# Two units' loads issued later, around the copies of odd values 20, in a fused attention and MLP kernel

## The chip, the cores and the metric

The kernel runs on one core of a Trainium2 chip. The metric is the device time of one execution in microseconds, as the median of several runs. One execution was also recorded by the profiler; its instructions, waits and transfers are what the profile and the trace show.

## The reference

The program computes sliding-window attention and then a two-layer perceptron over its output:

```python
scores = scale * np.matmul(q, k.transpose(0, 1, 3, 2))     # B, H, S, D = 8, 8, 576, 64
mask = np.abs(pos[:, None] - pos[None, :]) <= 32
scores = np.where(mask, scores, -1000000000.0)
attn = softmax(scores)
x = np.matmul(attn, v)            # -> (B * S, H * D) = (4608, 512)
h = x @ w_in                      # (512, 2048)
g = h * (1.0 / (1.0 + np.exp(-1.702 * h)))
out = g @ w_out                   # (2048, 512), float32
```

## The kernel before

**Units and tiles.** The 4608 rows are cut into 36 units of 128 rows (shifted by 32 for the queries) and 9 tiles of 512 rows, four units each. A unit goes through attention: its queries and keys are transposed, the scores are formed on TensorE (PE), exponentiated on ScalarE (ACT), masked on VectorE (DVE, `band`), multiplied with the values on PE (`values`), and divided by the row sums on DVE (`norm`), which gives x. A tile of four units then goes through both layers. Both layers use seven products in place of eight for a 2 by 2 split of the matrices (a Strassen scheme), so DVE forms sums of blocks: `x_sums` (xs) from the transposed x before layer 1, `g_sums` (gs) before layer 2.

**Where the data come from.** `fetch(u)` issues on POOL's queue (GpSimd) the loads of unit u's queries, unit u+1's keys and unit u+1's values, converting float32 to bfloat16 on the way; a load that crosses the end of a batch entry is two transfers. `turn(u)` issues on SP's queue the transposes by DMA of unit u's queries and unit u+1's keys. `odd_v(u)` copies on POOL the values into a second buffer, shifted by 64 rows: one copy reads unit u's values, the other unit u+1's. `x_T(u)` issues on SP the transpose of unit u's x. Finished rows of the output are stored from SP. Each queue works in the order in which its instructions are issued; an instruction whose data or buffer isn't ready holds back all behind it.

There are 5 buffers for staged queries, 5 for staged keys, 9 for values (`ve`), 5 for shifted values (`vo`) and 7 each for transposed queries and keys (`qT`, `kT`).

**The order.** The order on every engine is written out by hand. After an opening that treats the first tiles, the kernel alternates `front(t)` and `back(t)`. `front(t)` begins with the scores of units 4t+4 and 4t+5, goes on with layer 2 of an earlier tile, forms xs for tile t and ends with the scores of the two other units. `back(t)` has four groups n = 0 to 3, each of which calls `turn`, `fetch`, in groups 1 and 3 `values`, `norm` and `x_T` of two units, then `odd_v`, and then a group of layer 1 (`l1_group`, products 1, 7, 6, 2, 5, 4, 3) with layer-2 matmuls between its products. With u = 4t + 4, group n of `back(t)` turns unit u+n+4, fetches unit u+n+5 and copies the odd values of unit u+n+4. So in `back(2)` and `back(3)` (third and fourth tile, t = 2 and 3):

| group | before: turn | before: fetch | before: odd_v |
|---|---|---|---|
| (2, 2) | 18 | 19 | 18 |
| (2, 3) | 19 | 20 | 19 |
| (3, 0) | 20 | 21 | 20 |
| (3, 1) | 21 | 22 | 21 |

The first product that needs xs is product 7 of the tile's first group. The transposed x of units 14 and 15 belongs to the fourth tile, that of 18 and 19 to the fifth.

Of the kernel before, what the change touches and what calls it, by code (L numbers as in the profile page):

```python
# [26 lines left out]
class _Kernel:  # L27
# [706 lines left out]
    @staticmethod  # L734
    def do(fs, n=99):
        for _ in range(min(n, len(fs))):
            fs.pop(0)()
# [29 lines left out]
    def back(self, t):  # L767

        more = t + 1 < self.NT
        do, l2 = self.do, self.l2  # L770
        u = 4 * t + 4
        bands = [lambda i=i: self.band(u + i) for i in range(4)] if more else []
        dv = bands[0:2]
        for n in range(4):
            self.turn(u + n + 4)
            self.fetch(u + n + 5)
            if t == 2 and n in (1, 3):
                self.values(u + n - 1, "t")
                self.norm(u + n - 1)
                self.x_T(u + n - 1)  # L780
            elif more and n in (1, 3):
                do(l2, self.AHEAD[n][0])
                self.values(u + n - 1, "AC")
                self.norm(u + n - 1)
                if u + n < self.NU - 1:
                    self.x_T(u + n - 1)
                self.values(u + n, "t")
                self.norm(u + n)
                self.x_T(u + n)
                do(l2, self.AHEAD[n][1])  # L790
            if u + n + 4 < self.NU:
                self.odd_v(u + n + 4, self.nc.gpsimd)

            key = ("first", n) if t == 2 else ("last", n) if not more else n
            share = dict(zip((1, 7, 2, 4), self.SHARES.get(key, (3, 3, 5, 5))))

            def fill(i):
                do(l2, share[i])
                self.l2eng = self.nc.scalar
                if t == 2 and n in (1, 3) and i == 7:  # L800
                    self.values(u + n, "t")
                    if n == 3:
                        self.norm(u + n)
                        self.x_T(u + n)
                if i == 4:
                    do(dv, 2 if (t, n) == (2, 2) else 99)

            def side(i):
                if (t, n, i) == (2, 1, 0):
                    self.norm(u + n)  # L810
                    self.x_T(u + n)
                else:
                    do(dv, 1)

            self.l1_group(t, n, fill, side)
            dv += bands[2:4] if n == int(t == 2) else []
            dv += self.g_sums(t, 2 * n, 2)
        return dv
# [132 lines left out]
```

## Time and profile before

| | |
|---|---|
| median of 3 runs | 284.54 us (283.01 to 285.44) |
| profiled execution, its own time | 286.76 us |
| its span, first to last instruction | 285.0 us |
| granted clock of TensorE | 0.997 |
| busy: PE, DVE, ACT, POOL | 94%, 74%, 69%, 47% |
| read from HBM, written | 36.83 MB, 9.44 MB |

PE is TensorE's matmuls, PEld its weight loads, which overlap them. A row of a timeline gives the start, the duration, the engine, the line of the code, what is written and read, and in brackets how long the engine sat idle before and what it waited for. SPq and POOLq are the issues of transfers; a transfer lands some microseconds after its issue. A row of a window gives for each engine the busy time and, in brackets, the number of instructions, then the granted clock, the share of the DMA engines and the rate in GB/s.

### The profile page before, as it was taken

What the parts mean: (1) busy time and instruction counts of PE and PEld (TensorE: products, weight loads), DVE (VectorE), ACT (ScalarE), POOL (GpSimd) and SP (SyncE); (2) the same over time, 40 slices, a digit from 0 to 9 for tenths busy, and PEclk for the clock granted to TensorE, in tenths of its full rate; (3) what the DMA queues carried; (4) which work ended last, traced back from release to release, by engine and by line L of the source; (5) the groups of instructions that cost most, each with busy time, mean ns of one, the idle gap of its engine ahead of it and who ended that gap; (6) DMA issues with size and microseconds to landing.
All of it is one profiled execution on the core that took longest, in us unless ns stands there. A gap on an engine that the chain in (4) does not pass through costs nothing.

```text
span 285.0 us, 8889 instructions
## 1 busy us (share of the span) xinstructions
PE 269.0 (94%) x3648; PEld 221.8 (78%) x3648; DVE 212.3 (74%) x492; ACT 195.7 (69%) x343; POOL 133.4 (47%) x199
## 2 busy tenths in 40 slices
PE   1979999999999977999899999999999999999995
PEld 1568657776888865888788888888888888888883
DVE  3465697996987876797779787978788878945731
ACT  2586994899886594667866796689658865568411
POOL 8894785999696770738073908470310000000000
PEclk9999999999999999999999999999999999999998
DMA  8999999999999999999999999999923040201033
GB/s 89 168 205 198 178 207 159 187 121 156 170 133 138 211 124 179 117 163 145 174 112 199 153 177 65 183 158 198 147 58 74 24 113 20 74 2 74 2 110 114
DMA packets 150265, 37.61 MB, mean 132 GB/s; under 512 B 138064, under 2 KB 145872, under 8 KB 150224
## 3 DMA queue, kind: packets, MB, share of 16 engines
q0 software_dynamic: 106656, 18.42, 96.4%
q1 hardware_dynamic: 43120, 18.10, 36.8%
q8 instruction: 28, 0.46, 0.7%
q10 hardware_dynamic: 448, 0.52, 0.6%
q14 instruction: 13, 0.11, 0.2%
HBM read 36.83 MB, written 9.44 MB: 162 GB/s over the span
## 4 chain that ended last, share of the span: by engine, by line
PE 85%; DMA 6%; DVE 4%; ACT 2%; issue 1%; POOL 1%; ACTq 0%; DVEq 0%; POOLq 0%
PE h L70 37%; PE o L70 36%; DMA xT<-x 6%; PE pv L70 4%; PE sc L70 4%; DVE x L328 1%; PE tp L177 1%; DVE xs L388 1%; PE tp L244 1%; ACT kq L67 1%; POOL kq L152 1%; PE tp L344 0%; PE tp L356 0%; ACT L680 0%; PE tp L201 0%
## 5 line engine op out<-in xcount | busy, mean ns | idle before, releaser
L459 ACT ACTIVATE g<-h 128x512 f16<-128x512 f32 x128 | 72.2, 598 | 35.8 <-PE h L70 35.5
L222 POOL COPY vo<-ve 64x264 int32<-64x264 int32 x71 | 33.2, 468 | 65.1 <-PE pv L70 53.0
L70 PEld LDWEIGHTS <-g 128*128 128x128 f16 x576 | 54.5, 98 | 10.1
L70 PE MATMUL h<-xs,a 128*128 128x256 f16 x384 | 57.6, 272 | 2.6 <-DVE xs L388 1.8
L70 PEld LDWEIGHTS <-a 128*128 128x128 f16 x512 | 49.3, 98 | 12.8 <-DVE xs L388 3.7
L70 PE MATMUL o<-w,g 128*128 128x256 f16 (+1 forms) x320 | 55.0, 294 | 0.0
L70 PE MATMUL h<-xT,w 128*128 128x256 f16 (+1 forms) x368 | 53.6, 277 | 0.0
L70 PEld LDWEIGHTS <-w 128*128 128x128 f16 x496 | 47.7, 98 | 7.4
L70 PEld LDWEIGHTS <-gs 128*128 128x128 f16 x384 | 36.7, 98 | 4.8 <-issue 0.2
L290 ACT ACTIVATE p<-sc 128x512 bf16<-128x512 f32 x72 | 37.1, 616 | 3.5 <-PE sc L70 3.3
L70 PE MATMUL o<-b,g 128*128 128x256 f16 x256 | 38.3, 273 | 0.0
L70 PE MATMUL o<-b,gs 128*128 128x256 f16 x256 | 37.7, 273 | 0.0
L211 POOL DMA_DIRECT2D ve<-in_v_dram x40 | 34.3, 868 | 7.1 <-DMA w<-in_moe_w_out_dram 3.1
L472 DVE TENSOR_TENSOR h<-h,s 128x512 f32<-128x512 f32 x32 | 22.4, 699 | 19.5 <-PE h L70 19.3
L67 ACT COPY h<-h 128x512 f32<-128x512 f32 x32 | 18.7, 586 | 17.6 <-PE h L70 17.3
L328 DVE TENSOR_TENSOR x<-pv,rec 128x256 f16<-128x256 f32 (+1 forms) x52 | 27.4, 527 | 1.8
L141 POOL DMA_DIRECT2D qst<-in_q_dram x35 | 28.0, 803 | 1.3 <-issue 0.9
L478 DVE TENSOR_TENSOR h<-h,s 128x512 f32<-128x512 f32 x32 | 22.4, 699 | 6.2 <-PE h L70 5.9
L141 POOL DMA_DIRECT2D kst<-in_k_dram x31 | 26.5, 858 | 0.8 <-DMA w<-in_moe_w_out_dram 0.8
L298 DVE TENSOR_TENSOR p<-p,mask 128x1024 bf16<-128x1024 bf16 x32 | 22.8, 714 | 0.3 <-ACT p L290 0.3
L67 ACT COPY s<-h 128x512 f32<-128x512 f32 x32 | 19.0, 594 | 4.0 <-PE h L70 2.9
L70 PE MATMUL h<-xs,w 128*128 128x256 f16 x128 | 19.2, 273 | 0.0
(87 smaller groups left out, 339.7 us busy)
## 6 DMA issues: line engine op xcount, KB each, us to landing
out_dram<-o_sb SPq DMA_DIRECT2D x33, 256.0 KB, 4.6
ve<-in_v_dram POOLq DMA_DIRECT2D x32, 128.0 KB, 6.9
kst<-in_k_dram POOLq DMA_DIRECT2D x25, 128.0 KB, 6.8
qst<-in_q_dram POOLq DMA_DIRECT2D x21, 128.0 KB, 5.8
w<-in_moe_w_out_dram POOLq DMA_DIRECT2D x4, 512.0 KB, 11.2
w<-in_moe_w_in_dram POOLq DMA_DIRECT2D x3, 512.0 KB, 9.1
qst<-in_q_dram POOLq DMA_DIRECT2D x7, 96.0 KB, 6.3
kq<-in_q_dram POOLq DMA_DIRECT2D x2, 256.0 KB, 5.9
```

Of the source, the lines that this page charges most:

```text
L67: (eng.copy if eng is self.nc.scalar else eng.tensor_copy)(out, in_)
L70: self.nc.tensor.matmul(out, lhsT, rhs, start=start, stop=stop, skip_group_check=True)
L141: self.nc.gpsimd.dma_start(t[off:off + n], src[b, :, s:s + n, :].rearrange("h s d -> s h d"))
L152: self.nc.gpsimd.dma_start(self.stage["first"][0:n // j, :, at:at + j], src[0, :, lo:lo + n, :].rearrange("h (p j) d -> p h j d", j=j))
L211: self.nc.gpsimd.dma_start(t[off:off + n, :, :self.D], self.v[b, :, s:s + n, :].rearrange("h s d -> s h d"))
L222: eng.tensor_copy(*((words(vo[64:128]), words(self.ve[u % 9][64:128])), (words(vo[0:64]), words(nxt)))[i])
L290: self.nc.scalar.activation(p[:, eo].rearrange("k h s -> k (h s)"), sc[eo], AF.Exp, scale=self.scale)
L298: (eng or self.nc.vector).tensor_mul(pv, pv, msk.to_broadcast([128, 8, 2, SQ]))
L328: dve.tensor_mul(x[:, 4 * at:4 * (at + n), :].rearrange("p (b h) d -> p b h d", b=n), acc[:, :, :, :D], r.to_broadcast([128, n, 4, D]))
L459: act.activation(g[:, f, 256 * half:256 * half + 256], bank.rearrange("p (i n) -> p i n", i=2), AF.Gelu_apprx_sigmoid)
L472: dve.tensor_add(e, b, s7)
L478: dve.tensor_add(c, b, s7)
```

## The change

The loads of `fetch(20)`, issued in the last group of `back(2)`, are issued in the first group of `back(3)`, right ahead of the copies of `odd_v(20)`. Those of `fetch(21)` stay in that group, but go from ahead of these copies to behind them. `turn(20)` is written in the second group of `back(3)` in place of the first.

```diff
         for n in range(4):
-            self.turn(u + n + 4)
-            self.fetch(u + n + 5)
+            if (t, n) == (3, 1):
+                self.turn(20)
+            if (t, n) != (3, 0):
+                self.turn(u + n + 4)
+            if (t, n) not in ((2, 3), (3, 0)):
+                self.fetch(u + n + 5)
...
+            if (t, n) == (3, 0):
+                self.fetch(20)
             if u + n + 4 < self.NU:
                 self.odd_v(u + n + 4, self.nc.gpsimd)
+            if (t, n) == (3, 0):
+                self.fetch(21)
```

The order on POOL before and after (each fetch being three to five transfers, each odd_v two copies):

```
before: odd_v(18) fetch(20) odd_v(19) fetch(21) odd_v(20) fetch(22) odd_v(21)
after:  odd_v(18) odd_v(19) fetch(20) odd_v(20) fetch(21) fetch(22) odd_v(21)
```

The order of the instructions on PE, DVE, ACT and SP is the same before and after.

## The prediction

> **What bounds the kernel now.** I read the page first (engines, the slices of the clock and of the DMA engines, the queues), then the chain that ended last, then the timelines of PE, POOL and SP around the fourth tile, and last the times to landing of single transfers.
>
> ```profile
> span 285.0 us, 8889 instructions
> PE 269.0 (94%) x3648; PEld 221.8 (78%) x3648; DVE 212.3 (74%) x492; ACT 195.7 (69%) x343; POOL 133.4 (47%) x199
> PEclk9999999999999999999999999999999999999998
> DMA  8999999999999999999999999999923040201033
> q0 software_dynamic: 106656, 18.42, 96.4%
> q1 hardware_dynamic: 43120, 18.10, 36.8%
> ```
>
> TensorE is busy for 94% of the span at the full granted clock, so time can be won only where it waits. The DMA engines are taken almost without a break until three quarters of the span. The loads that POOL issues (queue 0) and the transposes and stores that SP issues (queue 1) share them.
>
> The kernel goes through its tiles at a nearly fixed pace, so I compare the same stretch in four tiles: from the first score matmuls of front(t) to the first matmul of product 7, which needs the sums xs of the tile's transposed x. The rows below are the fourth to the seventh tile (t = 3 to 6).
>
> ```profile
> 100.47:109.93 9.46, 6.12 (x137) 4.97 (x137) 4.99 (x13) 6.58 (x11) 4.77 (x7) 1.00 2.07 148
> 132.10:138.66 6.56, 5.91 (x137) 4.87 (x137) 4.39 (x12) 6.50 (x12) 2.85 (x4) 1.00 2.53 131
> 160.82:166.56 5.74, 5.74 (x137) 4.96 (x137) 4.90 (x14) 5.71 (x11) 2.81 (x5) 1.00 2.57 164
> 188.48:194.30 5.82, 5.82 (x138) 5.05 (x138) 5.02 (x14) 5.79 (x11) 2.57 (x3) 1.00 2.31 134
> ```
>
> The same 137 matmuls take 5.74 us where nothing is late. In the fourth tile they take 3.72 us more (9.46 - 5.74), in the fifth 0.82 us more. That is all that this change could remove: 4.5 us. What is late is seen in the timelines of PE and DVE, in the chain, and in the landing of the transpose whose issue lies in 100.5 to 101 us:
>
> ```profile
> 105.42 0.44 PE L70 MATMUL sc<-qT,kT 64*64 64x64 bf16 x22 [1.56 <-DMA kT<-kst]
> 109.93 0.61 PE L70 MATMUL h<-xs,a 128*128 128x256 f16 x4 [1.78 <-DVE xs L388]
> 109.45 0.43 DVE L388 TENSOR_TENSOR xs<-xT 128x512 f16<-128x512 f16 x1 [4.23 <-DMA xT<-x]
> ...
> 100.33 9.03 DMA xT<-x
> 129.87 8.21 DMA xT<-x
> ...
> xT<-x SPq DMA_TRANSPOSE x1, 9.0
> ```
>
> First a score waits 1.56 us for the transposed keys of unit 20, then product 7 waits 1.78 us for xs, whose input xT(15) was issued at 100.33 and landed 9.03 us later, at 109.36. The fifth tile has the same wait, smaller: xT(19), issued at 129.87, lands at 138.08.
>
> **The change.** No operation is added or removed; on PE, DVE, ACT and SP the order stays the same (turn(20) and turn(21) were neighbours on SP already). Only POOL's order changes: fetch(20), three issues, goes behind the two copies of odd_v(19), and fetch(21), five issues, behind the two copies of odd_v(20). POOL and SP before:
>
> ```profile
> 92.47 0.88 POOL L141 DMA_DIRECT2D qst<-in_q_dram  x1
> 94.21 0.89 POOL L211 DMA_DIRECT2D ve<-in_v_dram  x1
> 95.14 0.41 POOL L222 COPY vo<-ve 64x264 int32<-64x264 int32 x1
> 96.82 0.40 POOL L222 COPY vo<-ve 64x264 int32<-64x264 int32 x1 [1.28 <-DMA ve<-in_v_dram]
> 97.34 0.88 POOL L141 DMA_DIRECT2D qst<-in_q_dram  x1
> 98.20 1.39 POOL L141 DMA_DIRECT2D kst<-in_k_dram  x2
> 99.55 1.40 POOL L211 DMA_DIRECT2D ve<-in_v_dram  x2
> 101.00 1.23 POOL L222 COPY vo<-ve 64x264 int32<-64x264 int32 x2
> 102.21 1.36 POOL L141 DMA_DIRECT2D qst<-in_q_dram  x2
> 105.74 0.88 POOL L211 DMA_DIRECT2D ve<-in_v_dram  x1 [1.28 <-DMA qst<-in_q_dram]
> 115.26 0.86 POOL L222 COPY vo<-ve 64x264 int32<-64x264 int32 x2 [8.64 <-PE pv L70]
> ...
> 104.54 1.48 SPq L235 DMA_TRANSPOSE qT<-qst  x1
> 109.42 3.00 SPq L235 DMA_TRANSPOSE kT<-kst  x1
> 116.27 2.56 SPq L340 DMA_TRANSPOSE xT<-x  x2
> 119.69 2.16 SPq L493 DMA_DIRECT2D out_dram<-o_sb  x2
> 121.95 1.59 SPq L235 DMA_TRANSPOSE qT<-qst  x1
> 128.56 2.56 SPq L340 DMA_TRANSPOSE xT<-x  x2
> ```
>
> The issues at 92.47 to 95.1 are fetch(20), those from 97.34 fetch(21), those from 102.21 to 106.6 fetch(22). The copies at 95.14 and 96.82 are odd_v(19), the pair at 101.00 odd_v(20), the pair at 115.26 odd_v(21).
>
> **POOL, step by step.** The second copy of odd_v(19) still waits for v(20), loaded by fetch(19), until 96.82. So fetch(20) takes the place that fetch(21) had: q at about 97.3, k at 98.2, v at 99.1, done at 100.0. The first copy of odd_v(20) follows at once, but the second needs v(21), issued only 0.9 us before. Now POOL waits for a load that used to have a head start. Before, v(21) was issued at 94.21 and the pair at 101.00 took 1.23 us in place of 0.86, so it landed near 101.8, 7.6 us after its issue. Its time after the change is bounded by the quickest and the slowest v load near by (windows 146.5 to 147.4 and 100.5 to 101 us):
>
> ```profile
> ve<-in_v_dram POOLq DMA_DIRECT2D x1, 128.0 KB, 5.5
> ve<-in_v_dram POOLq DMA_DIRECT2D x1, 64.0 KB, 9.4
> ```
>
> I take 6.5 us, nearer the quick end since one unit's loads are under way in place of three: v(21) lands at 105.6, the copy ends at 106.0, fetch(21) runs from 106.0 to 109.7 (0.88 + 1.39 + 1.40) and fetch(22) to about 112.8. odd_v(21) was held until 115.26 by the value matmuls of unit 16 (8.64 us of idle). That idle time is the cover: POOL is back in step with 2.4 us to spare, or with none if TensorE comes as much earlier. By the bounds, fetch(21) starts between 105.0 and 108.9.
>
> **What the fourth tile wins.** While xT(14) and xT(15) are under way, queue 0 holds the 3 transfers of fetch(20) in place of up to 12 (3, 5 and 4 of fetch 20, 21 and 22, less those already landed). The time of xT(15) is bounded by 9.0 us (no relief) and by the transposes at 203 to 206 us, where no loads run:
>
> ```profile
> xT<-x SPq DMA_TRANSPOSE x1, 3.5
> xT<-x SPq DMA_TRANSPOSE x1, 7.0
> ```
>
> The second row is xT(23), issued within the window 158.2 to 159 us with one unit's loads around it and transposes of turns ahead of it, the state that the change makes. I take 7.0: landing at 107.3 in place of 109.36, so 2.1 us. The score's wait for kT(20) goes with the same relief. TensorE would then arrive 1.56 + 1.78 = 3.3 us earlier and wait for the last 1.3. Won up to here: 2.1 us, between 0 and 3.7.
>
> By the Trainium skill, page "DMA: Bandwidth & Descriptors", section "Queues, rings and completion order", each DMA engine goes round-robin between the queues it has work for. Taken alone this says that a shorter queue 0 does not help a transpose, only an empty one does, and by it the sum would be near 1 us; this would speak against most of the gain and stands as a rival below. The rows above (7.0 beside one fetch, 9.0 beside three) do not decide it, as the stores and turns around them differ too.
>
> **What the fifth tile gives back.** q(21) now lands near 113 and k(22), whose second half is issued at about 107.6, later than that. SP is in order: turn(21) waits for them, and behind it stand xT(16), xT(17), two stores, turn(22), turn(23), and then xT(18) and xT(19), which the fifth tile waits for. SP had 3.85 us of idle here (109.42 + 3.00 to 116.27), which hides the first part. The bounds for k (windows 88.5 to 91 and 98 to 99 us), and a row between (117.8 to 118.5 us, where fetch(23) and transposes run):
>
> ```profile
> kst<-in_k_dram POOLq DMA_DIRECT2D x1, 128.0 KB, 5.2
> kst<-in_k_dram POOLq DMA_DIRECT2D x2, 64.0 KB, 9.3
> kst<-in_k_dram POOLq DMA_DIRECT2D x1, 128.0 KB, 7.1
> ```
>
> With 7.1, k(22) lands at 114.7. From there SP needs 1.4 for kT(22), 2.7 for the xT pair, 1.1 for the stores (half the 2.16, an issue under load), and 6.6 for two turns (121.95 to 128.56): xT(18) goes out at about 126.5, 11.8 us after k(22), in place of 128.56. That is 2.1 us earlier, the same as TensorE has won, so the fifth tile's own 0.8 us stays and nothing is lost. The point at which it decides: k(22) landing at 116.8 gives all of it back. Later tiles ran without a wait (5.74, 5.82) and keep what is handed on.
>
> **Sum.** 2.1 us at the fourth tile, about 0.1 of the fifth tile's wait: 2.2 us. The profiled execution took 286.76 us with a span of 285.0, 2.2 above the median of 284.54 of the runs shown. 286.76 - 2.2 = 284.5 of its own time; against the median, 284.54 - 2.2 = 282.3 us.
>
> **Rivals.** (A) The relief is larger. Transposes fall to 5 or 6 us, both waits of the fourth tile and that of the fifth vanish: 3.72 + 0.82 = 4.5, 280.0 us. For it: with no loads they land in 3.5. Against it: the rows with loads beside the transpose are 7.0 and 9.0.
>
> (B) The change moves the loads but not the transposes. xT(14) and xT(15) still run beside fetch(20), which sits just where fetch(21) sat, and queue 0 is empty only from about 96.8 to 97.3 and for as short a time near 106. At twice the pace there (3.5 us alone, 7.0 beside loads), xT(15) comes at most 1 us earlier: 283.6 us. By the round-robin rule cited above this is the likely course. For it: the exchange is one fetch for another at the very time when the transposes go out.
>
> (C) Slower: the wait moves to SP. Place: turn(21), behind the late fetch(21), with xT(18) and xT(19) queued after it. With the slow bounds, v(21) in 9.4 us and k(22) in 9.3, k(22) lands at 119.8, xT(18) goes out at 131.6, 3.0 us later than now, and the fifth tile's wait grows by it whatever the fourth has won: 287.5 us. It decides from 116.8 on. For it: four fetches then follow each other from 106 to 121 us, and fetch(22)'s v row already shows POOL held 1.28 us by an earlier load. Against it: the slow times belong to a queue with three fetches in it, and at 99 to 107 there is one.
>
> **How the numbers follow.** Forecast 0.52, A 0.16, B 0.12, C 0.20. The forecast's own range is 1.0 to 3.4 us won, 281.1 to 283.5, as xT(15) takes 8.0 to 5.6 us. A change of 1%, 2.85 us, is about what a measurement of this kernel can tell from none. Not quite half of the forecast lies beyond it, since its two largest terms (7.0 and 7.1 us) each carry over a microsecond: 0.24 faster, 0.28 within. A is faster, B within, C slower but for 0.04. Faster 0.40, within 0.44, slower 0.16. The range of 280.2 to 286.2 leaves out the far end of A and of C.
>
> **What would show it.** In the changed profile: q(20) issued on POOL at about 97.3, a copy of L222 ended by a DMA of ve at about 105.6, fetch(21) behind it, fetch(22) done before 114. xT(15) landing at 107.3, the two PE waits of 1.56 and 1.78 us gone or under 1.3 together; the fourth tile's stretch near 7.4 us in place of 9.46. On SP kT(22) near 114.7, xT(18) near 126.5, and the fifth tile's stretch still near 6.5. Wrong if xT(15) still takes 9 us (B), or if the fifth tile's stretch grows beyond 8 us because SP stood at turn(21) (C).

## The result, and the profile after

| | before | after |
|---|---|---|
| median of 18 runs each | 284.58 us | 283.32 us |
| ratio, 95% interval | | 0.9959 [0.9941, 0.9977] |
| profiled execution, its own time | 286.76 us | 283.51 us |
| its span | 285.0 us | 281.7 us |

The changed kernel is faster by 0.41% in the ratio, 1.3 us between the medians; the forecast was 2.2 us (282.3). The two profiled executions differ by 3.3 us. Why these are not the same number is half of what the experiments had to find.

The page after, and the same stretch as before, from the first scores of front(t) to product 7, for the fourth to the seventh tile. The columns of the second view are the stretch, its length, then the busy time of PE, PEld, DVE, ACT and POOL, the clock, the DMA share and GB/s:

```profile
span 281.7 us, 8889 instructions
PE 268.9 (95%) x3648; PEld 222.5 (79%) x3648; DVE 212.4 (75%) x492; ACT 195.6 (69%) x343; POOL 132.0 (47%) x199
```

```profile
100.54:106.29 5.75, 5.75 (x138) 4.97 (x138) 5.43 (x14) 5.61 (x10) 1.40 (x3) 1.00 1.32 172
128.19:135.45 7.26, 6.11 (x137) 5.02 (x137) 4.32 (x12) 6.58 (x12) 3.52 (x5) 1.00 2.09 146
157.61:163.35 5.74, 5.74 (x137) 4.98 (x137) 4.90 (x14) 5.71 (x11) 2.81 (x5) 1.00 2.39 146
185.25:191.00 5.75, 5.75 (x138) 4.98 (x138) 4.91 (x14) 5.72 (x11) 2.44 (x3) 1.00 2.66 134
```

In this execution the fourth tile's wait is gone altogether: 9.46 us became 5.75. The fifth tile's wait has grown: 6.56 became 7.26. PE's busy time is the same (269.0 and 268.9), so the whole difference is waiting. In the chain that ended last only one transfer is left of the two shown before:

```profile
125.78 9.09 DMA xT<-x
```

It is the transpose of unit 19's x, and it is now slower than before the change (8.21).

POOL and SP after the change:

```profile
95.72 0.40 POOL L222 COPY vo<-ve 64x264 int32<-64x264 int32 x1 [0.20 <-DMA ve<-in_v_dram]
96.23 0.88 POOL L141 DMA_DIRECT2D qst<-in_q_dram  x1
...
104.88 0.50 POOL L222 COPY vo<-ve 64x264 int32<-64x264 int32 x1 [5.57 <-DMA ve<-in_v_dram]
105.39 0.88 POOL L141 DMA_DIRECT2D qst<-in_q_dram  x1
...
112.16 0.86 POOL L222 COPY vo<-ve 64x264 int32<-64x264 int32 x2
```

```profile
97.01 3.34 SPq L340 DMA_TRANSPOSE xT<-x  x2
...
111.55 1.19 SPq L235 DMA_TRANSPOSE kT<-kst  x1
112.84 2.62 SPq L340 DMA_TRANSPOSE xT<-x  x2
...
124.47 2.68 SPq L340 DMA_TRANSPOSE xT<-x  x2
```

fetch(20) starts at 96.23, behind the copy that waits for v(20). The second copy of odd_v(20) then waits 5.57 us for v(21), and fetch(21) follows at 105.39 in place of 97.34. POOL is back in step at 112.16, without idle time.

The travel (issue to landing) of kT(20), which SP issues just ahead of xT(14), before and after:

```profile
kT<-kst SPq DMA_TRANSPOSE x1, 8.0
kT<-kst SPq DMA_TRANSPOSE x1, 4.7
```

It landed at 105.38 before and at 100.40 after, 5.0 us earlier; xT(15) landed at 109.36 and 104.93, 4.4 us earlier. So most of what xT(15) wins has been won by the transposes ahead of it on SP's queue, those of turn(18) and turn(19) from 92 to 98 us, beside which the loads of fetch(20) ran before the change.

### The profile page after: what moved, and what is told of

The parts are those of the page before. It is cut to its first block, busy times and chain, and to the rows that moved or that the text cites. A ratio compares the mean times of both kernels' runs of the same rounds, so it can differ in the third digit from the quotient of the medians.

```text
span 281.7 us, 8889 instructions
## 1 busy us (share of the span) xinstructions
PE 268.9 (95%) x3648; PEld 222.5 (79%) x3648; DVE 212.4 (75%) x492; ACT 195.6 (69%) x343; POOL 132.0 (47%) x199
## 4 chain that ended last, share of the span: by engine, by line
PE 89%; DVE 3%; DMA 3%; ACT 2%; issue 1%; POOL 1%; POOLq 0%; DVEq 0%
PE o L70 38%; PE h L70 38%; PE sc L70 5%; PE pv L70 4%; DMA xT<-x 3%; DVE x L328 1%; PE tp L177 1%; PE tp L244 1%; ACT kq L67 1%; POOL kq L152 1%; ACT p L290 1%; PE tp L356 0%; ACT L680 0%; PE tp L344 0%; DVE xs L388 0%
## 5 line engine op out<-in xcount | busy, mean ns | idle before, releaser
L222 POOL COPY vo<-ve 64x264 int32<-64x264 int32 x71 | 31.8, 448 | 65.0 <-PE pv L70 45.4
```

Source lines behind the costliest of these rows:

```text
L222: eng.tensor_copy(*((words(vo[64:128]), words(self.ve[u % 9][64:128])), (words(vo[0:64]), words(nxt)))[i])
```

## The experiments

Two questions: where did the profile's 3.3 us go in the median, and by what mechanism does the place of a load move a transpose on another queue? The table collects all profiles. "Travel" is the time from issue to landing; the last two columns are the time from the first scores of one front(t) to those of the next, for the fourth and the fifth tile (27.65 us where nothing waits).

| kernel | fetch(20) from | behind v(20)'s landing | fetch(21) from | xT(15) travel | xT(19) travel | 4th tile | 5th tile | ratio |
|---|---|---|---|---|---|---|---|---|
| before | 92.47 | no | 97.34 | 9.0 | 8.2 | 31.63 | 28.72 | |
| b_again | 94.38 | no | 99.14 | 9.1 | 6.8 | 31.27 | 27.64 | |
| after | 96.23 | yes | 105.39 | 6.6 | 9.1 | 27.65 | 29.42 | 0.9959 |
| a_again | 98.96 | yes | 106.68 | 6.0 | 8.3 | 27.64 | 29.63 | |
| e1_only20 | 98.35 | yes | 100.95 | 6.6 | 7.7 | 27.70 | 27.64 | 0.9915 |
| e2_only21 | 93.87 | no | 106.51 | 8.1 | 8.6 | 29.16 | 29.74 | 0.9996 |
| e5_between | 96.37 | no | 101.70 | 8.7 | 6.5 | 30.82 | 27.64 | 0.9991 |
| e7_behind_v20 | 99.54 | yes | 102.55 | 5.8 | 8.3 | 27.72 | 28.49 | 0.9944 |
| e3_swap45 | 98.11 | yes | 107.57 | 7.3 | 5.0 | 29.57 | 27.64 | 0.9925 |
| e8_after_24 | 97.48 | yes | 106.47 | 6.7 | 5.9 | 28.02 | 27.63 | 0.9896 |
| e4_only20_24 | 99.87 | yes | 102.46 | 6.1 | 7.5 | 27.64 | 27.64 | 0.9908 |
| e6_only20to32 | 98.05 | yes | 100.64 | 5.9 | 7.0 | 27.65 | 27.64 | 0.9909 |

**Both kernels profiled once more (b_again, a_again).** No edit.

> The kernel before, unchanged, profiled once more. Theory 1 (the first profile of before caught an execution with a longer wait than usual in the fourth tile): its stretch from the first scores of front(3) to product 7 is well under the 9.46 us of the first profile, about 7.0 to 7.5, its own time near 284.6. Theory 2 (the first profile was typical, and the change gives its gain back later in most executions): the stretch is again 9.0 to 9.7, with xT(15) 9 us on its way.

> The changed kernel, unchanged, profiled once more. Theory 1: fourth tile's stretch 5.8 to 6.2 and the fifth's 6.5 to 7.5, own time near 283.3, as in the first profile of after (5.8 and 7.26). Theory 2: the fifth tile's stretch is about 9 us, since the usual execution gives back 2 us there.

Own times 285.15 and 283.48 us (the median of before beside them was 285.14). PE in b_again and in a_again, the rows of the scores and waits:

```profile
106.55 0.44 PE L70 MATMUL sc<-qT,kT 64*64 64x64 bf16 x22 [2.63 <-DMA kT<-kst]
...
131.58 0.70 PE L70 MATMUL sc<-qT,kT 64*64 64x64 bf16 x48
...
159.22 0.70 PE L70 MATMUL sc<-qT,kT 64*64 64x64 bf16 x48
```

```profile
127.90 0.70 PE L70 MATMUL sc<-qT,kT 64*64 64x64 bf16 x48
...
131.80 0.44 PE L70 MATMUL sc<-qT,kT 64*64 64x64 bf16 x22 [0.50 <-DMA kT<-kst]
135.37 0.61 PE L70 MATMUL h<-xs,a 128*128 128x256 f16 x4 [0.84 <-DVE xs L388]
...
157.53 0.70 PE L70 MATMUL sc<-qT,kT 64*64 64x64 bf16 x48
```

Neither theory held as a whole: theory 2 was right on b_again (a stretch of 9.11 us), theory 1 on a_again (7.47 us in the fifth tile). The fourth tile's wait of before came again: in b_again the tile takes 31.27 us from scores to scores. What the first profile of before had and b_again lacks is the fifth tile's wait of 1.1 us; which of the two is usual, two profiles can't show, but b_again's own time is that of the median. The changed kernel has a wait there in both profiles, 1.8 and 2.0 us. So against b_again the change wins 3.6 us in the fourth tile and gives back 1.8 to 2.0 in the fifth: 1.7 us between the two second profiles (285.15 - 283.48), against 1.3 us between the medians. Nor does the changed order always free the fourth tile: e3 and e8 below have the same order on POOL up to fetch(24), and their fourth tiles take 29.57 and 28.02 us.

**Each move alone (e1_only20, e2_only21).** The first moves fetch(20) only, the second fetch(21) only (in this and the following cuts of code, the lines that take the loads out of their old places are left out):

```diff
+            if (t, n) == (3, 0):        # e1: fetch(20) late, fetch(21) right behind it
+                self.fetch(20)
+                self.fetch(21)
             if u + n + 4 < self.NU:
                 self.odd_v(u + n + 4, self.nc.gpsimd)
+            if (t, n) == (3, 0):        # e2 instead: fetch(20) as before, fetch(21) late
+                self.fetch(21)
```

> Only fetch(20) moves behind the copies of odd_v(19); fetch(21) follows it at once, ahead of odd_v(20), as before. If it is the length of the load queue while xT(14) and xT(15) go out that matters, fetch(21) is still issued at about 99 to 102.5 and xT(15) keeps 8 us or more: ratio 0.998 to 1.002. If it is the head start (queue empty until 97), xT(15) takes about 7 and the ratio is that of the change, 0.996.

> Only fetch(21) moves behind the copies of odd_v(20); fetch(20) stays at 92.5. If the length of the queue matters: fetch(21) waits for v(21), near 100 to 101, so queue 0 is nearly empty from 100 to 103, xT(15) takes about 7, ratio 0.995 to 0.998, and without the late turn(21) the fifth tile keeps its small wait. If the head start matters: xT(15) keeps 8 to 9 us, ratio 0.999 to 1.001.

e1: 0.9915 [0.9884, 0.9945], no less than the whole change (0.9959 [0.9941, 0.9977]). e2: 0.9996 [0.9968, 1.0024], nothing. PE of e1 at the start of three tiles, and POOL where fetch(20) goes out:

```profile
100.53 0.70 PE L70 MATMUL sc<-qT,kT 64*64 64x64 bf16 x48
...
128.23 0.70 PE L70 MATMUL sc<-qT,kT 64*64 64x64 bf16 x48
...
155.87 0.70 PE L70 MATMUL sc<-qT,kT 64*64 64x64 bf16 x48
```

```profile
97.84 0.40 POOL L222 COPY vo<-ve 64x264 int32<-64x264 int32 x1 [2.35 <-DMA ve<-in_v_dram]
98.35 0.88 POOL L141 DMA_DIRECT2D qst<-in_q_dram  x1
```

27.70 and 27.64 us: both tiles run free. The gain is the move of fetch(20); the move of fetch(21) costs: the fifth tile takes 29.4 to 29.7 us in the three profiles in which fetch(21) is late and fetch(24) in its old place (after, a_again, e2), and 27.6 to 28.7 in the five that move neither (before, b_again, e1, e5, e7). In e2 the fourth tile still waits. e2 was meant to tell a short load queue from an empty one and does not: v(21) landed at 105.87, not at 100 to 101 as expected, and when xT(15) went out at 99.35, v(20) and all three loads of fetch(20) were still under way, four loads against at least five before. PE of e2:

```profile
105.15 0.44 PE L70 MATMUL sc<-qT,kT 64*64 64x64 bf16 x22 [0.70 <-DMA kT<-kst]
...
137.81 0.61 PE L70 MATMUL h<-xs,a 128*128 128x256 f16 x4 [1.65 <-DVE xs L388]
```

**Empty queue or only later (e5_between, e7_behind_v20).** One copy of odd_v(19) stands ahead of fetch(20) in both, fetch(21) stays ahead of odd_v(20) in both. In e5 it is the copy that needs nothing new; in e7 the one that waits for v(20), the last load of fetch(19):

```diff
+            if (t, n) == (2, 3):
+                self.odd_v(19, self.nc.gpsimd, (0,))    # e7: (1,)
+                self.fetch(20)
+                self.odd_v(19, self.nc.gpsimd, (1,))    # e7: (0,)
```

> fetch(20) goes between the two copies of odd_v(19), so it no longer waits for v(20) and is issued at about 95.5, between the time of before (92.5 to 94.4) and that of the change (96.2 or later); fetch(21) stays ahead of odd_v(20). Theory head start: kT(20), xT(14) and xT(15) still go out just behind or beside the loads, xT(15) takes 7 to 8.5 us, the fourth tile's excess is 1 to 2.5 us, ratio 0.993 to 0.998. If any issue behind the first copy is enough, xT(15) takes 6.6 and the ratio is 0.991.

> The mirror image of putting fetch(20) between the two copies of odd_v(19): now the copy that waits for v(20) stands ahead of fetch(20), and the other, which needs nothing new, behind it; fetch(21) stays ahead of odd_v(20). One copy stands ahead of the fetch in both kernels. Theory empty queue (transposes are quick when the load queue has run empty before the next loads are issued): fetch(20) is issued only once v(20) has landed, at 96 to 98.5; xT(15) takes 6 to 7 us, the fourth tile 27.6 to 28.2 us from scores to scores, ratio 0.989 to 0.994. Rival (a little later is enough or is of no use, whatever has landed): the same as with the other copy ahead, xT(15) 8 to 9 us, the fourth tile 30.8 us, ratio 0.999.

e5: 0.9991 [0.9966, 1.0016]; e7: 0.9944 [0.9903, 0.9984]. e5 wins nothing, less than its expectation of 0.993 to 0.998; its interval lies clear of e1's and overlaps e7's, so between e5 and e7 the profiles say more than the ratios. e7 is just outside the 0.989 to 0.994 expected. e5 issues fetch(20) at 96.37, by the clock as late as the changed kernel (96.23), but xT(15) takes 8.7 us, not 6.6. The difference is whether v(20) has landed. (The time alone is a weak comparison: all of POOL ran later in e5's profile, fetch(19) from 89.79 in place of 86.72.) POOL in e5, where v(20) lands only at 101.1, behind the issue, and in e7, where it lands at 98.88, just ahead of the copy, though the view puts that copy's wait down to PE:

```profile
96.37 0.88 POOL L141 DMA_DIRECT2D qst<-in_q_dram  x1
...
101.19 0.53 POOL L222 COPY vo<-ve 64x264 int32<-64x264 int32 x1 [2.20 <-DMA ve<-in_v_dram]
```

```profile
99.02 0.40 POOL L222 COPY vo<-ve 64x264 int32<-64x264 int32 x1 [5.47 <-PE h L70]
99.54 0.88 POOL L141 DMA_DIRECT2D qst<-in_q_dram  x1
```

The queues in the 3 us from the issue of xT(14) on (queue, packets, MB, time of its packets as a share of 16 engines, over 100% where several are under way), in e5 (99.40 to 102.40) and then e7 (97.98 to 100.98):

```profile
q0 software_dynamic: 1771, 0.22, 115.7%
q1 hardware_dynamic: 1366, 0.33, 63.1%
xT<-x SPq DMA_TRANSPOSE x2, 8.4
```

```profile
q1 hardware_dynamic: 1616, 0.39, 158.5%
q0 software_dynamic: 13, 0.00, 0.8%
xT<-x SPq DMA_TRANSPOSE x2, 5.5
```

With 1771 packets of loads beside them the two transposes take 8.4 us, with 13 they take 5.5. A copy that waits for the last load works as a gate: the next loads go out only when that one has landed, and the transposes that SP issues meanwhile run beside few loads or none.

Whether queue 0 must be empty is another matter. The same view of the changed kernel (97.01 to 100.01), where fetch(20) went out 0.8 us ahead of xT(14):

```profile
q0 software_dynamic: 1103, 0.14, 159.4%
q1 hardware_dynamic: 1756, 0.43, 75.4%
xT<-x SPq DMA_TRANSPOSE x2, 6.1
```

The Trainium skill says, page "DMA: Bandwidth & Descriptors", section "Queues, rings and completion order", that each DMA engine goes round-robin between the queues it has work for. Taken alone, that would make only an empty queue 0 a help. The traces don't show this: the travel of xT(15) goes with the number of loads under way at its issue. It is 9.0 us with at least five (before), 9.1, 8.7 and 8.1 with four (b_again, e5, e2), 6.6 and 7.3 with three (after, e3), 6.7 with two (e8), 6.6 and 5.9 with one (e1, e6), 6.0, 5.8 and 6.1 with none (a_again, e7, e4). So fewer loads and no loads are not told apart here, and these are single executions. In every profile that has both landings xT(15) landed 2.3 to 4.5 us behind kT(20); kT(20) itself landed at 104.9 to 106.5 us in before, b_again, e2 and e5, and at 100.4 to 102.6 in the others.

**The fifth tile (e3_swap45, e8_after_24).** e3 makes the change's exchange once more for fetch(24) and fetch(25); e8 is the change with only fetch(24) moved behind odd_v(23):

```diff
+            if t in (3, 4) and n == 0:
+                self.fetch(u + 4)          # t = 4: fetch(24), no longer in (3, 3)
+                if t == 4:
+                    self.fetch(u + 5)      # e8: ahead of odd_v(24); e3: behind it
```

> The change as it is, and the same exchange once more one tile later: fetch(24) behind the copies of odd_v(23), fetch(25) behind those of odd_v(24). Theory bunching (the late fetch(21) pushes later loads into each other, and xT(18) and xT(19) meet them): the fifth tile's wait shrinks from 1.8 to 2.0 us to under 0.5, but fetch(25) now comes late and the sixth tile gets a wait of 1 to 2 us; ratio 0.993 to 0.997. Rival (the fifth tile waits because SP was held at turn(21)): the fifth tile keeps its 1.8 to 2.0 us; ratio 0.996 or above.

> The change as it is, and in the fifth tile only fetch(24) moved behind the copies of odd_v(23), so that xT(18) and xT(19) go out beside fewer loads; fetch(21) is as late as in the change. Theory bunching: the fifth tile falls from 29.4 to 29.6 us between scores to 27.6 to 28.2, ratio 0.991 to 0.994. Rival (SP is late because of the late fetch(21), whatever loads run beside the transposes): xT(18) goes out under 3 us ahead of the scores and the fifth tile keeps 29 us or more, ratio 0.996.

e3: 0.9925 [0.9887, 0.9962]. Its fifth tile is free and the sixth takes 28.25 us, 0.6 more (1 to 2 were expected); but in its profile the fourth tile waited 1.9 us, which gave the queues time, so it does not decide alone. That wait also shows the limit of the gate: SP was late here (xT(15) went out at 99.86, in the changed kernel at 98.33), fetch(20) went out at 98.11 behind v(20), but ahead of xT(14) at 98.55, and xT(15) took 7.3 us. In e1, e4, e6 and e7 xT(14) went out first, and the fourth tile did not wait; but in the first profile of after fetch(20) went out first too, without a wait, so that order does not decide alone. PE of e3:

```profile
107.78 0.61 PE L70 MATMUL h<-xs,a 128*128 128x256 f16 x4 [1.44 <-DVE xs L388]
```

e8: 0.9896 [0.9833, 0.9959], the fifth tile 27.63 us:

```profile
128.47 0.70 PE L70 MATMUL sc<-qT,kT 64*64 64x64 bf16 x48
...
156.10 0.70 PE L70 MATMUL sc<-qT,kT 64*64 64x64 bf16 x48
```

It decides against the rival, since SP was not early: xT(18) goes out at 125.56, 2.9 us ahead of the scores at 128.47 (in the changed kernel 124.47 and 128.19, 3.7 us), and still nothing waits. The queues in the 3 us from that issue on, in the changed kernel (124.47 to 127.47) and in e8 (125.56 to 128.56):

```profile
q0 software_dynamic: 1559, 0.20, 101.9%
q1 hardware_dynamic: 1088, 0.26, 71.9%
xT<-x SPq DMA_TRANSPOSE x2, 8.6
```

```profile
q1 hardware_dynamic: 1662, 0.40, 104.9%
q0 software_dynamic: 41, 0.01, 26.1%
xT<-x SPq DMA_TRANSPOSE x2, 5.0
```

So the fifth tile pays for loads that are still under way when xT(18) and xT(19) go out. The last load of fetch(24) landed 5.3 and 6.5 us behind the issue of xT(18) in the two profiles of the changed kernel, 2.6 and 2.2 us behind it in the two of before. That a late fetch(21) does this by pushing the later loads into each other is argued, not shown: in e7, which has fetch(21) at 102.55, the fifth tile waited 0.8 us as well, with that load 6.1 us behind.

**Without either wait (e4_only20_24, e6_only20to32).** e1's move for fetch(20) and fetch(24), with fetch(21) and fetch(25) right behind them ahead of the copies; e6 does it for fetch(28) and fetch(32) too (t in 3 to 6):

```diff
+            if t in (3, 4) and n == 0:
+                self.fetch(u + 4)
+                self.fetch(u + 5)
             if u + n + 4 < self.NU:
                 self.odd_v(u + n + 4, self.nc.gpsimd)
```

> Only fetch(20) and, one tile later, only fetch(24) move behind the copies ahead of which they stood; fetch(21) and fetch(25) stay ahead of odd_v(20) and odd_v(24). Theory head start plus bunching: no wait in the fourth and fifth tile (27.6 to 27.8 us from tile to tile), ratio 0.988 to 0.991, at or a little under that of moving fetch(20) alone. Rival SP: a fifth tile's wait as in the changed kernel, ratio 0.995 or above.

> As moving fetch(20) and fetch(24) alone, and also fetch(28) and fetch(32) in the sixth and seventh tile, where the trace shows no wait of TensorE. Both theories: the same ratio as without these two, within 0.002, since there is nothing to win there; slower only if a later load there makes SP wait.

e4: 0.9908 [0.9876, 0.9940], median 282.50 us; both tiles 27.64 us. e6: 0.9909 [0.9869, 0.9950], median 281.95 us, the same within the intervals: nothing was to be won in the later tiles. e1, e4, e6 and e8 lie between 0.990 and 0.992 and can't be told apart; the interval of e1 [0.9884, 0.9945] ends below 0.9959, that of the changed kernel begins at 0.9941, so their order rests on the profiles more than on the ratios.

## Why the prediction was right, and where it was not

**POOL, step by step: right.** Forecast 97.3, 105.6, 106.0 and 112.8 for fetch(20), the copy that waits for v(21), fetch(21) and the end of fetch(22); measured 96.23, 104.88, 105.39 and 112.1.

**What the fourth tile wins: right in kind, too small.** 2.1 us forecast, 3.7 measured (9.46 to 5.75). xT(15) landed 4.4 us earlier: 2.4 us of that is its travel, 6.6 us where 7.0 was forecast, and 2.0 us its issue, at 98.33 in place of 100.33. The second part was not in the sum. SP's pair of issues starts at 97.01 in place of 98.64; 0.9 us of this was there already at the first transpose of turn(18) (91.70 and 92.64), before a moved load could act, and the rest comes from shorter issues of turn(18) and turn(19). The reason given, fewer transfers in queue 0, fits (three under way at xT(15)'s issue where before there were five or more), but no run separates it from the empty queue of (B). One row under it was misread: the transpose of 3.5 us near 203 us did not run without loads, as two loads of queries, issued at 200.09 and 200.86, landed at 204.47 and 204.88.

**What the fifth tile gives back: the step that failed.** I let xT(19)'s travel stand at 8.2 us and looked for the price on SP, at turn(21). SP was not held there: k(22) took 4.3 us where 7.1 was forecast (its first half; the landing of the second is not in the trace), kT(22) went out at 111.55, not 114.7, and xT(18) at 124.47, not 126.5. But xT(19)'s travel was 9.1 and 8.3 us beside the loads still under way. The term was 0.1 us won; it is 0.7 lost against the first profile of before, and 1.8 to 2.0 against the second.

**The sum against the median: right in part by luck.** The profiled execution lay 2.2 us above the median, which I said, and then I took the difference over unchanged. About 1.1 us of that excess was the fifth tile's wait, which b_again does not have; a wait that an execution lacks can't be won in it. Only 0.1 us of the sum rested on it, but it hid how much there was to lose. Against b_again the two errors have opposite signs: about 1.5 us too little in the fourth tile, 2 too much in the fifth, which leaves about 1.7 us of the 2.2, and 1.3 in the medians. That the time came so near is a matter of errors that cancel.

**The rivals.** (A) came true in the fourth tile only. (B) set the price too low: xT(15) took 6.6 and 6.0 us in the two profiles, where (B) allowed it to come 1 us earlier than 9.0. It was right on the empty time in the first of them (v(20) landed at 95.60, fetch(20) went out at 96.23), but took its pace from the misread row, and did not see that the transposes ahead of xT(14) would be quicker too. (C) had the right sign for the fifth tile but the wrong place, and it did not cost more than was won.

## What to carry to other kernels

Two queues on the same DMA engines: look at the loads that are still under way on one when an urgent transfer, or the transfers ahead of it, go out on the other. Loads issued behind it did little harm here (in e1 all eight of fetch(20) and fetch(21) followed xT(14), and the tile did not wait). Putting a bulk load behind an instruction that waits for the load before it keeps it from running beside them. With two loads chained so, look at where the later ones meet the next urgent transfers: here that cost 1.8 to 2.0 us, until fetch(24) was moved as well. And before a wait is entered in a sum, look at a second profile of the same kernel: here one wait of 1.1 us was there once and not again.

## What was not expected of the hardware

The issue of a transpose on SP does not always take the same time: kT(22) took 3.00 us at 109.42 before and 1.19 us at 111.55 after. Loads under way do not explain it, as there were six at the second of these; the cause stays open. A load of 64 KB took 3.3 to 12 us to land: v(22)'s halves 11.9 and 12.0 us in b_again, 3.5 and 3.3 us in e8.
